# Row norms in a fused attention and MoE kernel: the power on GpSimd replaced by Newton steps on VectorE, in groups and taken ahead

## Chip, cores, metric

One core of one Trainium2 chip. The metric is the device time of one execution in microseconds (us).

## The reference

Cosine attention over 8 batches x 12 heads x 448 rows x 64, followed by a two-layer MoE with a quick GELU.

```python
q_n = q / (np.linalg.norm(q, axis=-1, keepdims=True) + 1e-06)
k_n = k / (np.linalg.norm(k, axis=-1, keepdims=True) + 1e-06)
scores = np.matmul(q_n, k_n.transpose(0, 1, 3, 2)) / tau
...                                   # softmax over the last axis, times v
h = x @ w_in                          # x: 3584 x 768, w_in: 768 x 2048
g = h * (1.0 / (1.0 + np.exp(-1.702 * h)))
out = g @ w_out                       # w_out: 2048 x 768
```

## The kernel before

The kernel works on 48 pairs of heads, six pairs a batch. A pair takes two "steps". TensorE gets, in each step, scores, a share of MoE matmuls of an earlier batch, attention times v, another share, transposes (in the second step of a pair), another share. An engine takes its instructions in order, so whatever is emitted ahead of an instruction on the same engine can hold it: in the profile before, VectorE waited 3.01 us for a power at 310 us and ran an eviction only behind it, at 313.72, though that eviction's matmuls had ended at 309.45. Names of tiles in the profiles: n are sums of squares, nrm, rs and (in the new kernel) y the norms and their reciprocals, qks the scaled q and k, vt the cast v; tps are transposes in PSUM and qkT their copy; sp are scores, expT their exponentials; avp is attention times v in PSUM and av its eviction, the copy out of PSUM; mm is the PSUM tile of the MoE matmuls, th and gT make the GELU. tps and avp share one PSUM buffer, so transposes can start only when the av before them has been evicted (28 waits of TensorE, 45.7 us, in the profile before). The norms:

```python
def norm(x):                                     # one pair
    nrm = p_n.tile([P, 2, 2, C], FP32, name="nrm")
    nc.gpsimd.tensor_tensor(out=nrm, in0=n2s.pop(x), in1=half_c[...], op=ALU.pow)
    nc.vector.tensor_scalar(out=nrm, in0=nrm, scalar1=1e-6, scalar2=None, op0=ALU.add)
    rss[x] = p_n.tile([P, 2, 2, C], FP32, name="rs")
    nc.vector.reciprocal(out=rss[x], in_=nrm)
# (cut: the sums of squares before it: Square on ScalarE, tensor_reduce on VectorE;
#  the scale behind it: q and k times rs, on GpSimd)
```

The softmax denominators take a way through DRAM. Three pairs together: `den_out` (rows of av to DRAM), `den_in` (back as a dense tile, dnm), `den_rcp` (reciprocal rcg on VectorE, out to DRAM as rcp, back broadcast over partitions as rcb), then `normalise` (xT = av times rcb, on VectorE). All these transfers, the loads of q, k and v, and the stores are issued from one queue, SP's. The weights are issued from GpSimd's queue.

```python
for x in range(NPAIR):
    at(2 * (x - 6), load_qk, x)
    ...
    at(2 * (x - 2), norm, x)
    at(2 * (x - 2) + 1, scale, x, 1)
    ...
    if x % HP == HP - 1:
        at(2 * (x + 1) + 1 + 2 * d + 2, queue_moe, x // HP)
for i in range(4):
    at(-1 + 2 * i, load_w_in, i)
    at(9 + 2 * i, load_w_out, i)
```

## Time and profile before

| | before |
|---|---|
| time, median | 625.45 us |
| VectorE waiting for the power on GpSimd | 141.6 us |
| head: until the first MoE matmuls run at full pace | 114.8 us |
| middle: until TensorE has finished seven batches of MoE | 463.9 us |
| tail: last batch | 49.2 us |

The profiled execution took 627.9 from first to last instruction, so the three stretches sum to 627.9. They are read from TensorE's timeline. A wait in the profile is put down to the engine and instruction whose end came last. Line numbers (L119) differ between the two kernels; the names of the tiles are the same.

### The profile page before, as it was taken

The numbers are of one execution on the slowest core, as the hardware profiler recorded it, in microseconds if no ns is written. First come the engines' busy times: TensorE is split into PE (matmuls) and PEld (weight loads), VectorE is DVE, ScalarE is ACT, GpSimd is POOL, SyncE is SP. The second block draws the span as 40 slices with busy tenths as digits, with TensorE's granted clock in tenths as the row PEclk, the third lists the DMA queues.
The fourth block names the chain that finished last, engine by engine and source line by source line (L and its number), as shares of the span: only waits on it lengthen the run. The fifth ranks groups of instructions, "written<-read, shape, count | busy, mean of one in ns | idle before, by whom it ended". The sixth has DMA issues, their size and how long they took to land.

```text
span 627.9 us, 7945 instructions
## 1 busy us (share of the span) xinstructions
PE 496.5 (79%) x2816; PEld 243.0 (39%) x2816; DVE 294.5 (47%) x593; ACT 310.3 (49%) x473; POOL 281.7 (45%) x254
## 2 busy tenths in 40 slices
PE   0575555779979896998679896989589896898897
PEld 0122122344534453444334453445234452344454
DVE  3333353574456634555456635554556535451420
ACT  3553534465546554674546553664456553551331
POOL 5867565454535463355544463355643553300000
PEclk9966757799979998999979997999989997899899
DMA  9885957031522243143412252143412320002002
GB/s 226 155 168 124 186 122 158 8 104 44 172 60 68 66 125 110 45 110 88 144 44 68 77 141 83 45 111 96 135 45 67 85 74 26 2 24 86 13 25 76
DMA packets 55431, 56.61 MB, mean 90 GB/s; under 512 B 8064, under 2 KB 51936, under 8 KB 55392
## 3 DMA queue, kind: packets, MB, share of 16 engines
q1 hardware_dynamic: 50144, 49.82, 28.4%
q0 software_dynamic: 5248, 6.29, 6.6%
q8 instruction: 22, 0.36, 0.2%
q14 instruction: 17, 0.14, 0.1%
HBM read 51.20 MB, written 11.18 MB: 99 GB/s over the span
## 4 chain that ended last, share of the span: by engine, by line
PE 47%; DVE 26%; POOL 19%; issue 4%; ACT 2%; DMA 1%; SPq 0%; DVEq 0%; POOLq 0%
POOL nrm L119 18%; PE mm L297 16%; PE mm L257 15%; DVE xT L242 8%; PE avp L192 6%; DVE av L200 6%; PE sp L170 6%; PE tps L153 4%; DVE n L113 4%; DVE gT L267 3%; ACT th L266 2%; DVE qkT L159 2%; DVE rs L129 2%; DVE nrm L125 1%; DMA rcb<-rcp 1%
## 5 line engine op out<-in xcount | busy, mean ns | idle before, releaser
L119 POOL TENSOR_TENSOR nrm<-n,half_c 112x16 f32<-112x16 f32 x48 | 139.2, 2899 | 226.9 <-DVE n L113 226.9
L257 PE MATMUL mm<-xT,w_in 128*128 128x448 f16 x768 | 180.3, 379 | 46.3 <-DVE xT L242 42.2
L182 ACT ACTIVATE expT<-sp 112x896 f16<-112x896 f32 x192 | 170.1, 913 | 92.6 <-PE sp L170 92.4
L297 PE MATMUL mm<-w_out,gT 128*128 128x384 f16 x896 | 160.9, 326 | 0.6 <-DVE gT L267 0.6
L266 ACT ACTIVATE th<-mm 128x448 f16<-128x448 f32 x128 | 69.5, 543 | 143.2 <-PE mm L257 142.3
L257 PEld LDWEIGHTS <-w_in 128*128 128x128 f16 x768 | 75.2, 103 | 92.7 <-issue 38.9
L267 DVE SCALAR_TENSOR_TENSOR gT<-th,mm 128x448 f16<-128x448 f16 x128 | 76.8, 612 | 71.5 <-ACT th L266 71.4
L297 PEld LDWEIGHTS <-gT 128*128 128x128 f16 x896 | 83.9, 98 | 66.5 <-issue 11.5
L192 PE MATMUL avp<-expT,vt 112*128 112x448 f16 x384 | 99.3, 385 | 0.0
L200 DVE TENSOR_SCALAR av<-avp 65x448 f16<-65x448 f32 x96 | 58.1, 605 | 63.5 <-PE avp L192 63.0
L170 PE MATMUL sp<-qkT 64*112 64x448 f16 x384 | 68.4, 437 | 23.3 <-DVE qkT L159 21.7
L153 PE MATMUL tps<-ident,qks 112*128 112x112 f16 x384 | 33.2, 242 | 56.8 <-DVE av L200 45.7
L125 DVE TENSOR_SCALAR nrm<-nrm 112x16 f32<-112x16 f32 x48 | 8.4, 175 | 141.6 <-POOL nrm L119 141.6
L153 PEld LDWEIGHTS <-qks 112*128 112x128 f16 x384 | 28.5, 113 | 110.8 <-issue 56.3
L135 POOL TENSOR_TENSOR qks<-k,rs 112x512 f16<-112x512 f32 x48 | 50.0, 1042 | 34.4 <-DVE rs L129 27.2
L113 DVE TENSOR_REDUCE n<-sq 112x8 f32<-112x512 f32 x96 | 64.2, 670 | 2.6 <-ACT sq L108 2.0
L305 ACT ACTIVATE ost<-mm 128x384 f32<-128x384 f32 x56 | 27.4, 490 | 71.3 <-PE mm L297 71.1
L242 DVE TENSOR_TENSOR xT<-av,rcb 64x448 f16<-64x448 f16 x96 | 57.1, 594 | 7.1 <-DMA rcb<-rcp 5.9
L192 PEld LDWEIGHTS <-vt 112*128 112x128 f16 x384 | 37.2, 103 | 47.1 <-issue 21.2
L135 POOL TENSOR_TENSOR qks<-q,rs 112x512 f16<-112x512 f32 x48 | 51.9, 1081 | 0.0
L170 PEld LDWEIGHTS <-qkT 64*112 64x112 f16 x384 | 20.0, 143 | 63.1 <-DVE qkT L159 31.5
L159 DVE COPY qkT<-tps 128x896 f16<-128x896 f16 x48 | 29.8, 620 | 17.8 <-PE tps L153 16.8
(19 smaller groups left out, 126.0 us busy)
## 6 DMA issues: line engine op xcount, KB each, us to landing
q<-in_q_dram SPq DMA_DIRECT2D x48, 224.0 KB
k<-in_k_dram SPq DMA_DIRECT2D x48, 224.0 KB
v<-in_v_dram SPq DMA_DIRECT2D x48, 224.0 KB
rcb<-rcp SPq DMA_DIRECT2D x32, 168.0 KB
w_in<-in_moe_w_in_dram POOLq DMA_DIRECT2D x4, 768.0 KB, 8.6
w_out<-in_moe_w_out_dram POOLq DMA_DIRECT2D x4, 768.0 KB, 7.6
out_dram<-ost SPq DMA_DIRECT2D x7, 336.0 KB
out_dram<-ost SPq DMA_DIRECT2D x8, 288.0 KB
```

What stands on the lines that cost most here:

```text
L113: nc.vector.tensor_reduce(out=n2s[x][:, ti], in_=sqs.pop((x, ti)), axis=AX.X, op=ALU.add)
L119: nc.gpsimd.tensor_tensor(out=nrm, in0=n2s.pop(x), in1=half_c[:P, :, None, None].to_broadcast((P, 2, 2, C)), op=ALU.pow,)
L135: nc.gpsimd.tensor_tensor(out=qkss[x][:, ti].rearrange("p c j d -> p j c d"), in0=src, in1=rss[x][:, ti, :, :, None].to_broadcast((P, 2, C ...
L153: nc.tensor.transpose(out=tps[:, ti, c * P : (c + 1) * P], in_=qks[:, ti, c].rearrange("p j d -> p (j d)"), identity=ident[:P, :P],)
L170: nc.tensor.matmul(out=sp[:, j, :S], lhsT=qkT[64 * j : 64 * (j + 1), 1, c * P : (c + 1) * P], rhs=qkT[64 * j : 64 * (j + 1), 0, :], start= ...
L182: nc.scalar.activation(out=e, in_=sps.pop((x, c))[:, :, :S], func=AF.Exp, scale=inv_tau, **kw)
L192: nc.tensor.matmul(out=ps, lhsT=vts[x % 4][:, c, j], rhs=exps[x, c][:, j], start=(c == 0), stop=(c == C - 1),)
L200: nc.vector.tensor_scalar(out=avs[x][:n, j], in0=ps[:n], scalar1=AV_SCALE, scalar2=None, op0=ALU.mult)
L242: nc.vector.tensor_tensor(out=xT[r], in0=av[r, j], in1=rcbs[x // GRP][r, x % GRP], op=ALU.mult)
L257: nc.tensor.matmul(out=ps[:, :S], lhsT=w_in_sb[:, kk, 128 * m : 128 * (m + 1)], rhs=xTs[b, kk], start=(kk == 0), stop=(kk == KT1 - 1),)
L267: nc.vector.scalar_tensor_tensor(out=gT[:, m], in0=th, scalar=1.0, in1=ps[:, :S], op0=ALU.add, op1=ALU.mult,)
L297: nc.tensor.matmul(out=ps[:, :NW], lhsT=gT[:, kk, 128 * t : 128 * (t + 1)], rhs=w_out_sb[:, kk, cols], start=(kk == 0), stop=(kk == KT2 - 1),)
```

## The change

Intent: take the power off GpSimd, so that VectorE need not wait; do the norms of three pairs in one block, several pairs ahead of use; spread MoE matmuls over the remaining steps.

```diff
-    def norm(x):
-        nc.gpsimd.tensor_tensor(out=nrm, in0=n2s.pop(x), in1=half_c[...], op=ALU.pow)
-        nc.vector.tensor_scalar(out=nrm, in0=nrm, scalar1=1e-6, ..., op0=ALU.add)
-        nc.vector.reciprocal(out=rss[x], in_=nrm)
+    def norm(grp):                                  # 1, 2 or 3 pairs
+        a = n2s.pop(grp).rearrange("p g a b c -> p (g a b c)")
+        nc.vector.tensor_scalar(out=y.bitcast(I32), in0=a.bitcast(I32),
+            scalar1=-0.5, scalar2=RS_MAGIC, op0=ALU.mult, op1=ALU.add)
+        for ca, cb in ((-RS_A, RS_B), (-0.5, 1.5)):
+            nc.vector.scalar_tensor_tensor(out=t, in0=y, scalar=ca, in1=y, ...)
+            nc.vector.tensor_tensor(out=t, in0=t, in1=a, op=ALU.mult)
+            nc.vector.scalar_tensor_tensor(out=y, in0=t, scalar=cb, in1=y, ...)
+        nc.vector.tensor_scalar(out=t, in0=y, scalar1=1e-6, scalar2=1.0, ...)
+        nc.vector.reciprocal(out=t, in_=t)
+        nc.vector.tensor_tensor(out=y, in0=y, in1=t, op=ALU.mult)
 (cut)
-        at(2 * (x - 6), load_qk, x)
-            at(2 * (x - 3) + ti, square, x, ti)
-        at(2 * (x - 2), norm, x)
+        s = sq_step.get(x, 2 * (x - 6))            # squares three pairs earlier
+        if x >= HP:
+            at(s - 5, load_qk, x)
+        if x == group_of[x][-1]:
+            at(s + (1 if x < HP else 2), norm, group_of[x])
 (cut)
-        at(-1 + 2 * i, load_w_in, i)
-        at(9 + 2 * i, load_w_out, i)
+        at(3 + 2 * i, load_w_in, i)
+        at(11 + 2 * i, load_w_out, i)
 (cut: the first six pairs' loads before the loop, one scale moved to VectorE)
-        jobs = later.pop(s, [])
+        jobs = sorted(later.pop(s, []), key=...)   # squares, reduces, norms first
+        step_ns = max(todo / max(2 * NPAIR + 4 - s, 1), 0)     # was 3150
```

The first of the ten operations reads the bits of the fp32 sum as an integer and makes a first guess of one over the square root; two rounds of three operations (Newton steps) refine it; the last three bring in the 1e-6.

More of the change, by code (lines that the diff above doesn't have):

```diff
@@ L10 @@
 FP16 = mybir.dt.float16
+I32 = mybir.dt.int32
 AF = mybir.ActivationFunctionType
@@ L16 @@
 MM2_NS = 163
-STEP_NS = 3150
+RS_MAGIC = float(0x5F1FFFF9)
+RS_A, RS_B = 0.703952253, 0.703952253 * 2.38924456
 AV_SCALE = 2.0**-11
@@ L74 @@
     ctx.enter_context(tc.manual_schedule())
-    half_c = const.tile([128, 2], FP32)
-    nc.vector.memset(half_c, 0.5)
     ident = const.tile([128, 128], FP16)
@@ L110, in reduce, with scale @@
     def reduce(x, ti):
-        if ti == 0:
-            n2s[x] = p_n.tile([P, 2, 2, C], FP32, name="n2")
+        grp = group_of[x]
+        if grp not in n2s:
+            n2s[grp] = p_n.tile([P, len(grp), 2, 2, C], FP32, name=f"n2_{len(grp)}")
         nc.vector.tensor_reduce(
-            out=n2s[x][:, ti], in_=sqs.pop((x, ti)), axis=AX.X, op=ALU.add
-        )
-    def norm(x):
-        nrm = p_n.tile([P, 2, 2, C], FP32, name="nrm")
-        nc.gpsimd.tensor_tensor(
-            out=nrm,
-            in0=n2s.pop(x),
-            in1=half_c[:P, :, None, None].to_broadcast((P, 2, 2, C)),
-            op=ALU.pow,
-        )
+            out=n2s[grp][:, x - grp[0], ti],
+            in_=sqs.pop((x, ti)),
+            axis=AX.X,
+            op=ALU.add,
+        )
+    def norm(grp):
+        n = len(grp)
+        a = n2s.pop(grp).rearrange("p g a b c -> p (g a b c)")
+        y = p_n.tile([P, 16 * n], FP32, name=f"y_{n}")
+        t = p_n.tile([P, 16 * n], FP32, name=f"t_{n}")
+        nc.vector.tensor_scalar(
+            out=y.bitcast(I32),
+            in0=a.bitcast(I32),
+            scalar1=-0.5,
+            scalar2=RS_MAGIC,
+            op0=ALU.mult,
+            op1=ALU.add,
+        )
+        for ca, cb in ((-RS_A, RS_B), (-0.5, 1.5)):
+            nc.vector.scalar_tensor_tensor(
+                out=t, in0=y, scalar=ca, in1=y, op0=ALU.mult, op1=ALU.mult
+            )
+            nc.vector.tensor_tensor(out=t, in0=t, in1=a, op=ALU.mult)
+            nc.vector.scalar_tensor_tensor(
+                out=y, in0=t, scalar=cb, in1=y, op0=ALU.add, op1=ALU.mult
+            )
         nc.vector.tensor_scalar(
-            out=nrm, in0=nrm, scalar1=1e-6, scalar2=None, op0=ALU.add
+            out=t, in0=y, scalar1=1e-6, scalar2=1.0, op0=ALU.mult, op1=ALU.add
         )
-        rss[x] = p_n.tile([P, 2, 2, C], FP32, name="rs")
-        nc.vector.reciprocal(out=rss[x], in_=nrm)
-    def scale(x, ti):
+        nc.vector.reciprocal(out=t, in_=t)
+        nc.vector.tensor_tensor(out=y, in0=y, in1=t, op=ALU.mult)
+        yv = y.rearrange("p (g a b c) -> p g a b c", g=n, a=2, b=2)
+        for x in grp:
+            rss[x] = yv[:, x - grp[0]]
+    def scale(x, ti, eng=None):
         if x not in qkss:
@@ L134, in scale @@
         src = (q32, k32)[ti].pop(x)
-        nc.gpsimd.tensor_tensor(
+        (eng or nc.gpsimd).tensor_tensor(
             out=qkss[x][:, ti].rearrange("p c j d -> p j c d"),
@@ L314 @@
     streams = []
+    todo = (B - 1) * (KT1 * KT2 * MM1_NS + 7 * KT2 * MM2_NS)
     def fill(ns):
+        nonlocal todo
         while ns > 0 and streams:
             try:
-                ns -= next(streams[0])
+                n = next(streams[0])
+                ns -= n
+                todo -= n
             except StopIteration:
@@ L345, in at @@
         later.setdefault(s, []).append((f, a))
+    sq_step = {0: -4, 1: -3, 2: -2, 3: 0, 4: 2, 5: 3, 6: 5, 7: 6, 8: 7, 9: 9, 10: 10, 11: 11}
+    groups = [(0,), (1, 2), (3, 4), (5,)]
+    groups += [tuple(range(g, g + GRP)) for g in range(HP, NPAIR, GRP)]
+    group_of = {x: g for g in groups for x in g}
     for x in range(NPAIR):
-        at(2 * (x - 6), load_qk, x)
-        at(2 * (x - 5), load_v, x)
-        for ti in range(2):
-            at(2 * (x - 3) + ti, square, x, ti)
-            at(2 * (x - 3) + ti + 1, reduce, x, ti)
-        at(2 * (x - 2), norm, x)
+        s = sq_step.get(x, 2 * (x - 6))
+        if x >= HP:
+            at(s - 5, load_qk, x)
+            at(2 * (x - 4), load_v, x)
+        for ti in (1, 0):
+            late = 0 if x < HP or ti == 1 else 1
+            at(s + late, square, x, ti)
+            at(s + late + (1 if x > 0 else 0), reduce, x, ti)
+        if x == group_of[x][-1]:
+            at(s + (1 if x < HP else 2), norm, group_of[x])
         at(2 * (x - 2) + 1, scale, x, 1)
-        at(2 * (x - 2) + 1, scale, x, 0)
+        at(2 * (x - 2) + 1, scale, x, 0, *([nc.vector] if x == 0 else []))
         at(2 * (x - 2) + 1, cast_v, x)
@@ L368 @@
     for i in range(4):
-        at(-1 + 2 * i, load_w_in, i)
-        at(9 + 2 * i, load_w_out, i)
+        at(3 + 2 * i, load_w_in, i)
+        at(11 + 2 * i, load_w_out, i)
+    for x in range(HP + 2):
+        if x < HP:
+            load_qk(x)
+        if x >= 2:
+            load_v(x - 2)
     make_identity(nc, ident)
@@ L380 @@
         x, half = s // 2, s % 2
-        jobs = later.pop(s, [])
+        jobs = sorted(
+            later.pop(s, []), key=lambda j: {square: 0, reduce: 1, norm: 2}.get(j[0], 3)
+        )
+        step_ns = max(todo / max(2 * NPAIR + 4 - s, 1), 0)
         if 0 <= x < NPAIR:
@@ L384 @@
             exp(x, 2 * half)
-        fill(STEP_NS * 0.33)
+        fill(step_ns * 0.33)
         if 0 <= x < NPAIR:
@@ L391 @@
             f(*a)
-        fill(STEP_NS * 0.33)
+        fill(step_ns * 0.33)
         if half == 1 and 0 <= x + 1 < NPAIR:
@@ L396 @@
             f(*a)
-        fill(STEP_NS * 0.34)
+        fill(step_ns * 0.34)
     fill(1e9)
```

## The prediction

> **What bounds the kernel now.** I read the waits summed over the whole run first, because the change removes one wait.
>
> ```profile
> POOL nrm L119 <- DVE n L113: 226.9, 46, 9.5
> DVE nrm L125 <- POOL nrm L119: 141.6, 48, 5.1
> PE tps L153 <- DVE av L200: 45.7, 28, 4.5
> PE mm L257 <- DVE xT L242: 42.2, 10, 6.1
> ```
>
> The power on GpSimd waits 226.9 us for its sums of squares, so GpSimd is not full. It matters because VectorE waits for it: 48 waits, 141.6 us, about 2.95 us each, the length of one power. VectorE takes its instructions in order, so whatever stands behind that wait stands still too. The timeline near 310 us shows it:
>
> ```profile
> 310.41 2.90 POOL L119 TENSOR_TENSOR nrm<-n,half_c 112x16 f32<-112x16 f32 x1 [3.28 <-DVE n L113]
> ...
> 313.34 0.17 DVE L125 TENSOR_SCALAR nrm<-nrm 112x16 f32<-112x16 f32 x1 [3.01 <-POOL nrm L119]
> 313.55 0.25 DVE L129 RECIPROCAL rs<-nrm 112x16 f32<-112x16 f32 x1
> 313.72 0.56 DVE L200 TENSOR_SCALAR av<-avp 128x448 f16<-128x448 f32 x1
> ...
> 314.20 2.27 DVE L242 TENSOR_TENSOR xT<-av,rcb 64x448 f16<-64x448 f16 x2
> ...
> 316.53 0.53 PE L257 MATMUL mm<-xT,w_in 128*128 128x448 f16 x1 [6.13 <-DVE xT L242]
> ```
>
> A PSUM eviction (av) and two normalisations (xT), ready earlier, run only after the power, and TensorE loses 6.13 us. The chain of waits agrees: the power alone is 18.1% of it (114 us). Next, stretches of 20 us (columns: engine busy us, granted clock, DMA share, GB/s):
>
> ```profile
> 40.00:60.00 20.00, 11.45 (x54) 4.46 (x54) 7.66 (x18) 8.97 (x12) 12.92 (x12) 0.62 0.66 147
> 220.00:240.00 20.00, 20.00 (x134) 10.73 (x133) 7.82 (x18) 11.87 (x19) 10.53 (x10) 1.00 0.45 128
> 300.00:320.00 20.00, 11.79 (x69) 5.50 (x67) 10.42 (x21) 8.47 (x13) 11.55 (x10) 0.86 0.37 107
> 580.00:600.00 20.00, 17.00 (x80) 8.29 (x80) 9.81 (x19) 7.06 (x13) 0.00 (x0) 0.91 0.06 22
> ```
>
> These are three regimes. In the head (to the first MoE matmul at 115 us) there is attention alone: no engine is full, and a pair takes 9.5 us. In the middle, stretches of the second MoE matmul beside attention fill TensorE completely, while stretches around the start of the first MoE matmul do not. The tail is the last batch's MoE on TensorE.
>
> [...]the power takes 2,899 ns for 16 elements a partition, a tensor_scalar of the same shape 175 ns. [...]here tensor_scalar to reciprocal starts 0.21 us apart (313.34 to 313.55), so about full length each.[...]
>
> **The change, part by part.**
>
> *Removed.* 48 powers: 139.2 us of GpSimd (281.7 falls to some 141), and the 141.6 us of VectorE waits. The 96 small VectorE operations go too (8.4 + 12.1 = 20.5 us).
>
> *Added.* Ten small VectorE operations a group, 18 groups: 14 of three pairs, two of two, two of one. [...]The reciprocal measures 253 ns at 16 elements and 289 at 24 (fp16), so 4.5 ns an element, some 397 ns at 48 (estimate). [...]for one pair 9 x 0.175 + 0.253 = 1.83[...]. VectorE goes from 294.5 to 294.5 - 20.5 + 39 + 0.6 (one scale moved to it) = about 314 us. They wait only for VectorE itself, and from the seventh pair on lie three to four pairs ahead of their use, so nobody waits for their result[...].
>
> *Moved.* Squares and loads go earlier, the weights later. *The balanced MoE share does next to nothing*: the instruction order of TensorE shows the same 18 first or 21 second MoE matmuls a step (half a pair) in both kernels up to step 89. The loop runs on until its nanoseconds are used up, and 1,050 or 1,040 ns both mean six of 189 or seven of 163. Only from step 90 are there 19 instead of 18. I give it 0 to 1 us.
>
> **Head: 115 to about 80 us.** First scores come at 16.2 us now; loads and the two-pair group still stand ahead of the first qkT copy, so about 15. Then 9.5 pairs to the first MoE step. A pair needs of ScalarE 4 x 0.913 + 2 x 0.627 = 4.9 us; of VectorE 2 x 0.67 + 2 x 0.605 + 0.62 + 2 x 0.594 + 0.85 = 5.2 us; of TensorE at the low clock about 6.2 us (1.00 per four scores, 1.6 per four attends, 0.92 for transposes). So about 6.3 us instead of 9.5: 15 + 60 = 75. DMA is the check:
>
> ```profile
> q1 hardware_dynamic: 12788, 11.52, 36.4%
> q0 software_dynamic: 5248, 6.29, 34.5%
> ```
>
> That is the DMA view of the first 120 us: plain loads 0.364 x 120 / 11.52 = 3.8 us a MB, weights 41 us in all. By the first MoE step the new order wants q and k of 16 pairs and v of 12 (10.1 MB, 38 us) and has asked for all weights: 79 us. So DMA takes over as the limit of the head at nearly the same place. I take 80, a gain of 35.
>
> **Middle: 464 to about 410 us** (115.0 to 578.7, where TensorE runs out of the seventh batch). Floor of TensorE from full stretches: four scores 0.52, four attends 0.76, eight transposes 0.39 in two steps, MoE matmuls 0.190 and 0.164 us. A batch of 12 steps: 12 x 1.28 + 6 x 0.39 = 17.7, plus 96 x 0.190 + 112 x 0.164 = 36.6: 54.3 us against 70 now (the xT groups before the first MoE matmul repeat at 244.8, 314.3, 385.0, 454.4). Seven batches of MoE and 79 steps of attention: 256 + 116 = 372. Now 92 us are lost beyond that. I keep 38: per batch 2.5 us for the first MoE matmul waiting on the last xT (in the same step, behind a reduce), 1.5 for a norm block that falls into it, 0.8 of clock; and 4 us for the steps with no or hardly any MoE (51, 52, 75, 76), whose order is unchanged. A step of the first MoE matmul needs 6 x 3 x 0.19 + 1.47 = 4.9 us of TensorE and about 4.5 of VectorE (three gT of 0.61, a reduce, an eviction, half a copy, one xT[...]), so VectorE has little slack there. That is why I keep as much.
>
> **Tail: 49 us, unchanged**: five of waiting on the last denominators' way through DRAM, 44 of MoE.
>
> Sum 80 + 410 + 49 = 539 on the profiled run; the timed runs lie 2 us under the profile's span. **Prediction 537 us**, 14% under 625.45.
>
> **Rivals.** *(1) VectorE becomes the bound.* For: 4.5 of 4.9 us a step in the first MoE phase, and the blocks come in bursts. Against: it is 47% busy over all and idles in the second phase (7.82 of 20). If it ruled those phases, losses would be nearer 65 us: about 565. *(2) The head is held by transfers*: weights now sit in 14 steps that run faster; 0.82 to 1.00 DMA share in 20 to 100 us says it can happen. If plain loads starve behind weights, the head is 90 to 95: about 550. *(3) The power was only one of parallel waits*, so evictions and normalisations still keep TensorE waiting, and the low clock stays in the head: 9.5 falls only to 7.5 us a pair, middle losses 60: about 575. *(4) All goes well*: losses of 15 to 20 us, head 72: about 510. Full stretches such as 220 to 240 speak for it.
>
> **Range and chances.** Head 72 to 92, middle 390 to 435, tail 47 to 53; not all at the same end: 512 to 566 holds 8 in 10. To miss 2% (613) would need nearly all of the gain to turn into a new wait, so faster 0.97, same 0.02, slower 0.01.
>
> **What would show it.** GpSimd busy near 141 us and no long wait of VectorE on it;[...] VectorE busy near 314. First MoE matmul at 75 to 90 us, with DMA share near full before it. A batch taking 58 to 61 us instead of 70. TensorE's granted clock above 0.93 in the middle. The remaining waits of TensorE on xT at 2 to 3 us instead of 6. I am wrong if the head stays above 95 us, if the batch period stays above 64 us, or if VectorE waits on DMA or ScalarE take the place of the power.

What the prediction said of the hardware without a trace of this case behind it is cut out of it, and the cuts are marked. Terms of its sums are gone with it, namely the durations of VectorE's operations over two and three pairs. The ten operations came to 39 us over the whole run, the 39 in 294.5 - 20.5 + 39 + 0.6, and the about 4.5 us of VectorE a step holds a share of them. The changed kernel measured 41 us in all, 2.28 us for the ten operations of a block of three pairs, and 208 ns for one of its two-input operations.

## The result

560.18 us median (559.58 to 561.48, 4 runs) against 625.53 us (4 runs) beside it. The ratio is 0.8956, 95% interval 0.8927 to 0.8985. A ratio is the mean time of one kernel's fast runs over that of the other's of the same rounds, so it is not quite the ratio of the medians.

| | before | forecast | after |
|---|---|---|---|
| head, us | 114.8 | 80 | 106.3 |
| middle, us | 463.9 | 410 | 400.3 |
| tail, us | 49.2 | 49 | 51.2 |
| GpSimd busy, us | 281.7 | 141 | 140.7 |
| VectorE busy, us | 294.5 | 314 | 303.2 |

The waits summed over the run, kernel after (us in total, times, longest us):

```profile
POOL qks L156 <- DVE y L147: 170.8, 18, 13.8
POOL vt L167 <- PE avp L213: 124.7, 47, 4.4
DVE av L221 <- PE avp L213: 111.5, 51, 4.0
...
PE mm L278 <- DVE xT L263: 18.6, 14, 4.7
...
DVE xT L263 <- DMA rcb<-rcp: 13.1, 4, 5.5
```

VectorE's 141.6 us of waiting for GpSimd are gone. GpSimd now waits for VectorE (170.8 us) and TensorE (124.7), and runs ahead all the same: TensorE waited for its scales once, 10.1 us before the first transposes. The matmul's wait on xT fell from 42.2 us to 18.6. One line is small in the sum and large in one place: xT waits for the transfer rcb, 13.1 us in four waits against 5.9 in two before; 7.5 of them now lie in the head. Three stretches of 20 us (busy us of TensorE's matmuls, its weight loads, VectorE, ScalarE and GpSimd; granted clock, DMA share, GB/s) show where:

```profile
40.00:60.00 20.00, 13.98 (x62) 4.76 (x61) 10.82 (x25) 14.10 (x21) 6.22 (x8) 0.74 0.83 172
60.00:80.00 20.00, 5.87 (x32) 2.63 (x31) 9.92 (x25) 6.19 (x10) 5.16 (x9) 0.66 1.04 215
...
220.00:240.00 20.00, 17.98 (x109) 8.62 (x109) 14.29 (x33) 13.23 (x22) 5.12 (x7) 1.00 0.23 69
```

In the middle, from 120 to 500 us, TensorE is now busy 95% of the time (82 to 100% in stretches of 20 us), at the full clock in all but one of them (0.91). The stretch from 60 to 80 us has TensorE busy for only 5.87 us, with the DMA engines full (share 1.04). The timeline there, kernel after:

```profile
60.69 0.81 POOL L363 DMA_DIRECT2D w_out<-in_moe_w_out_dram  x1
...
65.35 1.35 SPq L250 DMA_DIRECT2D rcb<-rcp  x2
...
66.01 0.81 POOL L363 DMA_DIRECT2D w_out<-in_moe_w_out_dram  x1
...
71.85 0.38 DVE L263 TENSOR_TENSOR xT<-av,rcb 64x448 f16<-64x448 f16 x1 [5.53 <-DMA rcb<-rcp]
...
75.43 0.62 DVE L221 TENSOR_SCALAR av<-avp 128x448 f16<-128x448 f32 x1
...
76.10 0.90 PE L174 MATMUL tps<-ident,qks 112*128 112x112 f16 x8 [9.26 <-DVE av L221]
...
79.78 1.61 DVE L263 TENSOR_TENSOR xT<-av,rcb 64x448 f16<-64x448 f16 x2
81.42 0.62 DVE L180 COPY qkT<-tps 128x896 f16<-128x896 f16 x1
82.10 0.99 PE L191 MATMUL sp<-qkT 64*112 64x448 f16 x4 [5.09 <-DVE qkT L180]
```

Two quarters of w_out are asked for around the moment that the first rcb is. The delay had begun a transfer earlier: SP's queue stood 6.7 us for rcp before it could ask for rcb. VectorE stands for rcb (5.53 and 1.97 us), the eviction av stands behind xT, and TensorE loses 9.26 us. It loses 5.09 more before the scores, because two reduces, a norm block (77.28 to 79.86) and two more xT stand ahead of the qkT copy. Scores of successive pairs begin at 14.5, 19.3, 29.2, 39.1, 46.0, 55.0, 62.4, 82.1, 89.2 and 94.7 us. So periods without a disturbance are about 7.1 us (6.9, 7.4, 7.1). Those with a block of norms ahead of the qkT copy or of an eviction are 10.0, 9.9 and 9.1. The one with the stall, which has a norm block too, is 19.7. The first (4.8) and the last (5.5) are shorter.

### The profile page after: what moved, and what is told of

It reads as the page before. It is cut to its first block, busy times and chain, and to the rows that moved or that the text cites. A ratio compares the mean times of both kernels' runs of the same rounds, so it can differ in the third digit from the quotient of the medians.

```text
span 557.8 us, 7958 instructions
## 1 busy us (share of the span) xinstructions
PE 474.8 (85%) x2816; PEld 236.2 (42%) x2816; DVE 303.2 (54%) x677; ACT 310.5 (56%) x473; POOL 140.7 (25%) x205
## 4 chain that ended last, share of the span: by engine, by line
PE 65%; DVE 18%; DMA 10%; issue 2%; ACT 2%; SPq 2%; DVEq 0%; ACTq 0%
PE mm L318 23%; PE mm L278 21%; PE avp L213 12%; PE sp L191 8%; DVE xT L263 4%; DVE av L221 3%; DVE n L114 3%; DMA rcp<-rcg 3%; DMA rcb<-rcp 3%; DVE qkT L180 2%; DMA v<-in_v_dram 2%; DVE gT L288 2%; PE tps L174 2%; ACT th L287 2%; DMA q<-in_q_dram 1%
## 5 line engine op out<-in xcount | busy, mean ns | idle before, releaser
L278 PE MATMUL mm<-xT,w_in 128*128 128x448 f16 x768 | 170.2, 362 | 18.6 <-DVE xT L263 18.6
L278 PEld LDWEIGHTS <-w_in 128*128 128x128 f16 x768 | 72.4, 99 | 86.8 <-issue 29.5
L156 POOL TENSOR_TENSOR qks<-k,y 112x512 f16<-112x512 f32 x48 | 50.5, 1053 | 188.4 <-DVE y L147 170.8
L191 PE MATMUL sp<-qkT 64*112 64x448 f16 x384 | 64.2, 411 | 28.6 <-DVE qkT L180 25.5
L167 POOL CAST vt<-v 112x256 f16<-112x256 f32 x96 | 37.2, 401 | 130.8 <-PE avp L213 124.7
L174 PE MATMUL tps<-ident,qks 112*128 112x112 f16 x384 | 28.9, 223 | 31.1 <-DVE av L221 21.1
L156 POOL TENSOR_TENSOR qks<-q,y 112x512 f16<-112x512 f32 x47 | 49.2, 1048 | 0.0
L174 PEld LDWEIGHTS <-qks 112*128 112x128 f16 x384 | 25.3, 103 | 54.0 <-issue 39.3
L263 DVE TENSOR_TENSOR xT<-av,rcb 64x448 f16<-64x448 f16 x96 | 39.3, 409 | 14.7 <-DMA rcb<-rcp 13.1
L108 ACT ACTIVATE sq<-k 112x512 f32<-112x512 f32 x48 | 30.3, 632 | 6.7 <-DMA k<-in_k_dram 5.2
## 6 DMA issues: line engine op xcount, KB each, us to landing
w_out<-in_moe_w_out_dram POOLq DMA_DIRECT2D x4, 768.0 KB, 10.1
```

Source lines behind the costliest of these rows:

```text
L156: (eng or nc.gpsimd).tensor_tensor(out=qkss[x][:, ti].rearrange("p c j d -> p j c d"), in0=src, in1=rss[x][:, ti, :, :, None].to_broadcast ...
L174: nc.tensor.transpose(out=tps[:, ti, c * P : (c + 1) * P], in_=qks[:, ti, c].rearrange("p j d -> p (j d)"), identity=ident[:P, :P],)
L191: nc.tensor.matmul(out=sp[:, j, :S], lhsT=qkT[64 * j : 64 * (j + 1), 1, c * P : (c + 1) * P], rhs=qkT[64 * j : 64 * (j + 1), 0, :], start= ...
L263: nc.vector.tensor_tensor(out=xT[r], in0=av[r, j], in1=rcbs[x // GRP][r, x % GRP], op=ALU.mult)
L278: nc.tensor.matmul(out=ps[:, :S], lhsT=w_in_sb[:, kk, 128 * m : 128 * (m + 1)], rhs=xTs[b, kk], start=(kk == 0), stop=(kk == KT1 - 1),)
```

## The experiments

Two theories of the head stood at first. T: transfers, the weights above all, are in the way of rcb. V: the order on VectorE holds it, with norm blocks in a phase in which TensorE has no MoE matmuls to fill with. A second question was what the middle owes to which part of the change. "Head" and "middle" are as in the table, from each run's profile.

| run | time, us | ratio to before | head, us | middle, us |
|---|---|---|---|---|
| changed kernel | 560.2 | 0.896 | 106.3 | 400.3 |
| e1 weights by memset (wrong result) | 558.5 | 0.893 | 105.1 | 400.4 |
| e2 weights as before | 560.6 | 0.896 | 108.2 | 400.3 |
| e3 first normalise late | 557.4 | 0.892 | 111.1 | 399.5 |
| e4 Newton in place | 579.2 | 0.926 | 96.3 | 431.9 |
| e5 quarter of the weights (wrong result) | 555.1 | 0.888 | 101.6 | 399.8 |
| e6 reduces behind the copy | 561.3 | 0.898 | 108.8 | 399.3 |
| e7 norms pair by pair, ahead | 588.6 | 0.941 | 112.4 | 424.4 |
| e8 power ahead | 639.1 | 1.021 | 127.8 | 454.4 |
| e9 fixed share | 561.0 | 0.897 | 108.3 | 400.5 |
| e10 power ahead, 10 input buffers | 556.5 | 0.890 | 108.0 | 395.9 |
| e11 head rearranged | 553.9 | 0.886 | 101.4 | 400.5 |
| e12 the same as e11, 10 input buffers | did not build | | | |
| e12b the same as e11, 9 input buffers | 554.8 | 0.887 | 101.9 | 400.5 |

The profiled run of e3 took 562.9 us, over 5 us more than the median, so its head is not typical.

### e1, e5: weights without transfers

```diff
 e1:
-        nc.gpsimd.dma_start(out=w_in_sb[:, :, n], in_=moe_w_in...)
+        nc.gpsimd.memset(w_in_sb[:, :, n], 0.03)          # w_out likewise
 e5:
-    w_in_sb = wpool.tile([128, KT1, DFF], FP16, name="w_in")
+    w_in_sb = wpool.tile([128, KT1, 512], FP16, name="w_in")
-                    lhsT=w_in_sb[:, kk, 128 * m : 128 * (m + 1)],
+                    lhsT=w_in_sb[:, kk, 128 * (m % 4) : 128 * (m % 4 + 1)],
                                        # w_out likewise; one load of each, not four
```

> The changed kernel with both weights filled by GpSimd memsets instead of transfers (wrong result on purpose; the memsets cost GpSimd some 2 to 3 us each, eight of them). Theory T, transfers: 41 us of weight transfers crowd the head, the first rcb lands late and VectorE stands for it in order (9.3 us of TensorE idle at 66 to 76 us). Then the first MoE matmuls reach full pace at 85 us or earlier instead of 106, and the whole takes about 540 us. Theory V, VectorE's order: reduces and norm blocks stand ahead of evictions and qkT copies in a phase where TensorE has no filler, whatever the DMA does. Then full pace comes at 100 us or later and the whole takes 554 or more.

> The changed kernel with a quarter of each weight loaded and used four times over (wrong result on purpose; no engine gets extra work, unlike the memsets of e1, which kept GpSimd busy and once held a small VectorE operation for 5.8 us). Theory T: weight transfers hold the head through the late rcb (pair period 19.7 us instead of 7.1 around 62 to 82 us). Then full pace of the first MoE matmul comes at 95 us or before instead of 106, and the whole takes 546 to 550 us. Theory V: VectorE's order holds it anyway. Then 103 us or later, 557 or more.

e1 hardly moved (558.5 us), but it was not clean. Its timeline, VectorE and GpSimd alone:

```profile
31.88 2.66 POOL L357 MEMSET w_in<- 128x3072 f16 x1
...
34.05 5.81 DVE L127 TENSOR_SCALAR y<-n 112x16 int32<-112x16 int32 x1
...
34.50 1.05 POOL L156 TENSOR_TENSOR qks<-k,y 112x512 f16<-112x512 f32 x1
35.50 1.05 POOL L156 TENSOR_TENSOR qks<-q,y 112x512 f16<-112x512 f32 x1
...
36.48 0.75 POOL L167 CAST vt<-v 112x256 f16<-112x256 f32 x2
...
37.16 2.66 POOL L357 MEMSET w_in<- 128x3072 f16 x1
```

An operation that took 0.17 us with GpSimd idle (at 6.24 us in the changed kernel) took 5.81 us. A memset (2.66 us) was running when it began; then GpSimd went through two scales, two casts and a memset without a gap. The operation ended (39.86) when the last memset did (39.82). The memsets kept GpSimd busy and so made a cost of their own. By what means GpSimd held the operation was not shown.

e5 gives no engine extra work. It came to 555.1 us, head 101.6. So three quarters of the weights' transfers cost the head about 5 us, and V's 557 and T's 550 are both missed: T is right in kind and small in size. Its timeline shows the rest of the stall:

```profile
67.54 0.38 DVE L263 TENSOR_TENSOR xT<-av,rcb 64x448 f16<-64x448 f16 x1 [0.31 <-DMA rcb<-rcp]
68.30 1.19 DVE L263 TENSOR_TENSOR xT<-av,rcb 64x448 f16<-64x448 f16 x3 [0.37 <-DMA rcb<-rcp]
69.51 0.62 DVE L221 TENSOR_SCALAR av<-avp 128x448 f16<-128x448 f32 x1
...
70.19 0.55 PE L174 MATMUL tps<-ident,qks 112*128 112x112 f16 x8 [2.35 <-DVE av L221]
...
75.35 1.00 PE L191 MATMUL sp<-qkT 64*112 64x448 f16 x4 [4.61 <-DVE qkT L180]
```

VectorE waits 0.7 us for rcb here, and the pair (62.8 to 75.35 us) still takes 12.6 us instead of 7.1. So of the stall's 19.7 us about 7 are the late transfers, and 5.5 are VectorE's own order: six xT and a norm block ahead of an eviction and a copy.

### e2, e3, e11: when weights and the first normalisation come

```diff
 e2:
-        at(3 + 2 * i, load_w_in, i)
-        at(11 + 2 * i, load_w_out, i)
+        at(-1 + 2 * i, load_w_in, i)
+        at(9 + 2 * i, load_w_out, i)
 e3 (p_av from 6 to 10 buffers):
-                at(s + 2 * d + 1 + i // 2, normalise, x - GRP + 1 + i)
+                at(s + 2 * d + 1 + i // 2 + (5 if x < GRP else 0), normalise, ...)
 e11 = e3 and:
+        at(-1 + 2 * i, load_w_in, i)
+        at((6, 7, 20, 22)[i], load_w_out, i)
```

> The changed kernel with the weights asked for at the steps of the kernel before (w_in from step -1, w_out from step 9), so 4 and 2 steps earlier. Theory T with room: DMA stood idle from 27 to 33 us, earlier weights use that, fewer of them stand in front of the first rcb: 546 to 556 us. Theory V, or T with DMA full anyway: within 3 us of 560. Worse than 560 if early weights delay q and k.

> The changed kernel with the normalisation of the first three pairs five steps later (nobody needs them before the first MoE matmul) and 10 buffers of av so that they can wait. Theory T as an in-order wait: the 5.5 + 2.0 us of VectorE waiting on rcb at 66 to 74 us, with the 9.3 us gap of TensorE, leave: 549 to 554 us. If the transfers limit the head by their sheer volume, the time comes back as waits of ScalarE on q and k or GpSimd on v: 558 or more.

> The changed kernel with weights kept away from the first denominators (w_in from step -1 as before, two quarters of w_out at steps 6 and 7, the other two at 20 and 22), and the first normalisation late, with 10 buffers of av. If late rcb and dnm transfers behind weights, and VectorE's wait for them in order, are what the head lost against the forecast of 80 us: the stall of 12.6 us and most of the 5 us of the run with quarter weights leave, full pace of the first MoE matmul at 90 to 94 us, 544 to 549 us. If the head's serial order and norm blocks limit it: 553 or more.

Earlier weights alone do nothing (560.6 us, as V, or T with DMA full, expected): the pair with the stall still takes 20.6 us, since quarters of w_out still lie around the first rcb. The late normalisation alone brings 557.4 us with a wide interval (0.887 to 0.898), short of the 549 to 554 expected. Its profile shows that pair at 10.1 us, but the next group's denominators then came late:

```profile
87.94 0.30 DVE L245 RECIPROCAL rcg<-dnm 112x24 f16<-112x24 f16 x1 [7.04 <-DMA dnm<-den]
```

VectorE stood 7.04 us for dnm instead. The wait had found another transfer of the same chain. Both edits together, with the weights kept clear of the denominators, take the stall away: the pair periods from 58 us on are 7.0, 9.3 (with a norm block), 6.9 and 6.9 us. The time is 553.9 us, and the head 101.4. That is the lowest median of all runs, with a correct result. It is above the 544 to 549 expected for late transfers, and fits the 553 or more expected for serial order and norm blocks. Of the 10.4 us that this pair gained, 2.8 came back in the pair that now starts at 46.3 us, where VectorE waits 2.04 us for the first dnm, and 1.5 each in the last pair and between it and full pace. What is left in the head is for the most part not this stall.

### e6: norm blocks behind the copy

```diff
-        for f, a in jobs[: len(jobs) // 2]:
+        cut = len(jobs) // 2 if s >= 19 else 0
+        for f, a in jobs[:cut]:
```

> The changed kernel with all side jobs of steps before 19 (reduces, norm blocks, scales) behind the transposes and the qkT copy instead of half of them ahead. Theory V: pair periods of 9.9, 9.9 and 9.1 us around the norm blocks of the head fall towards the 7.1 us of pairs without one, together 7 to 9 us: 551 to 554 us. Theory T: the stall on rcb takes the gain back: 558 or more.

561.3 us, no gain. The first scores came 2.9 us earlier (11.6), but a later norm block met GpSimd's scales and weight issues and took from 30.3 to 35.7 us instead of about 2; three of the operations in it took 0.91 to 1.07 us beside GpSimd, where 0.17 was usual. One period grew to 13 us, and the stall on rcb stayed (19.2 us). So the run does not tell what the norm blocks cost in a clean head. That stays open.

### e4, e7: Newton without the rest, and without the grouping

e4 is the kernel before with the ten VectorE operations in place of the power, pair by pair; e7 is the changed kernel with single pairs from the seventh on:

```diff
 e7:
-    groups += [tuple(range(g, g + GRP)) for g in range(HP, NPAIR, GRP)]
+    groups += [(g,) for g in range(HP, NPAIR)]
```

> The kernel before with the power replaced by the exponent guess and two Newton steps on VectorE, pair by pair and in the old place; loads, squares, weights and MoE share stay as before. If the wait for the power was the cost and taking the norms ahead in threes adds little: 570 us or less, with VectorE busy about 294 - 20 + 88 - some 18 of faster xT = 344 us. If taking ahead and grouping carry half of the gain: 590 or more.

> The changed kernel with the norms from the seventh pair on taken pair by pair, still ahead: 42 blocks of 1.83 us instead of 14 of 2.3, so VectorE gets 45 us more. If VectorE has slack in the middle and being ahead is what counts: 563 us or less. If VectorE is close to the bound beside the first MoE matmul: 567 to 577, that is 1 to 2.5 us a batch, and grouping is what counts.

e4: 579.2 us, between the two expectations. Its middle is 431.9 us; the Newton steps in the old place already bring 32 of the middle's 64 us, and the head falls to 96.3, lower than in the changed kernel. VectorE was busy for 363.7 us, not the 344 expected, because xT stayed at 0.587 us. The head: nine pair periods take 72.2 us there against 80.2 in the changed kernel, and VectorE does not wait for rcb, although all weights are loaded and more had been moved by 66 us (13.7 MB against 11.4). So the weights alone do not make the stall. The loads of q, k and v, the squares and the norm blocks differ as well, and no run separates them, nor does one join this head to the grouped norms of the middle. e7: 588.6 us, worse than expected, middle 424.4. VectorE has some 48 us more work than in the changed kernel (351.4 against 303.2), and the middle is 24 us longer. So VectorE is close enough to being the limit that half of its extra work shows, and the grouping is worth those 24 us. Between e4 and e7 (ahead or in place, both single pairs) the middle differs by only 7.5 us.

### e8, e10: the power again, but ahead

Groups of three on GpSimd, with VectorE's two operations taken two steps later from the tenth pair on:

```diff
+        nc.gpsimd.tensor_tensor(out=t, in0=a, in1=half_c[...], op=ALU.pow)   # norm
+        ...                                                    # norm_b, two steps on
+        nc.vector.tensor_scalar(out=t, in0=t, scalar1=1e-6, ..., op0=ALU.add)
+        nc.vector.reciprocal(out=y, in_=t)
 e10 = e8 and:
-    p_in = pool("p_in", 6)
+    p_in = pool("p_in", 10)
```

> The changed kernel with the power on GpSimd again, for the groups of three, and the two VectorE operations behind it taken two steps later (from the tenth pair on), so that VectorE need not stand for it. If the wait in VectorE's order was the whole cost of the power: within 12 us of the changed kernel, 560 to 572. If the power as such costs, by holding scales on GpSimd (some 8.5 us for 48 elements) or VectorE's two-input operations (xT at 0.59 us instead of 0.41): 580 or more.

> The run with the power ahead (e8, 639 us) with 10 instead of 6 input buffers. There the load queue waited 210 us for GpSimd, whose scales stood behind 8 us powers, and so the denominators' transfers behind it came late and VectorE waited 77 us on them. Theory B, the wait moved into the load queue: with free buffers the queue no longer waits, and the time falls to 565 to 580 us. Theory P, the power itself: still 610 or more.

e8: 639.1 us, 1.6 to 2.5% slower than the kernel before, and far above the 560 to 572 expected if VectorE's wait was the whole cost of the power. VectorE no longer waits for the power for long. It waits for a transfer, and the load queue waits for GpSimd. From the waits of e8, first VectorE's, then the load queue's own:

```profile
DVE rcg L239 <- DMA dnm<-den: 77.0, 13, 14.1
```

```profile
SPq L95 <- POOL vt L161: 209.8, 17, 19.3
```

A power over 48 elements takes 8.0 us. The scales stand behind it on GpSimd, the input buffers come free late, the load that wants one blocks the SP queue, and the denominators' transfers stand behind that load. e10 tests this by adding buffers alone. The time fell by 83 us to 556.5, below the 565 to 580 expected. In the load queue's waits of e10, that of L95 on GpSimd is gone, and VectorE's on dnm fell from 77.0 us to one wait:

```profile
DVE rcg L239 <- DMA dnm<-den: 3.5, 1, 3.5
```

The chain is shown. The run also shows more: with the wait removed at both ends (but for 26.5 us of VectorE on the power, in five waits at the head's first groups), the power on GpSimd is as fast as the Newton steps. Its row in e10, by form:

```profile
L129 POOL TENSOR_TENSOR t<-n,half_c 112x48 f32<-112x48 f32 x14 | 112.1, 8010 | 171.6 <-DVE n L116 171.6
```

112.1 us of powers over three pairs are there, and the middle is 395.9 us.

### e12b: the control for the buffers

> The rearranged head (e11, 553.9 us, Newton steps on VectorE) with 9 instead of 6 input buffers (10 do not fit beside the 10 av buffers); nothing else differs. A control for the run with the power ahead and 10 input buffers (556.5 us). If buffers help only where GpSimd is slow to free them, this is within 2 us of 554 (the load queue waits for GpSimd only some 9 us in all in the changed kernel), and the power ahead is then as fast as the Newton steps. If the buffers alone speed up the Newton version as well: 550 or less, and the comparison of the two was unfair by that much.

```diff
 e12b = e11 and:
-    p_in = pool("p_in", 6)
+    p_in = pool("p_in", 9)
```

e12, with 10 input buffers beside e11's 10 av buffers, did not build: the on-chip memory was too small (the last pool wanted 9 kB a partition, 5.47 were left). e12b has 9: 554.8 us against 553.9, within the 2 us expected. More input buffers do nothing for the Newton version, so e10 against the changed kernel (0.890 against 0.896) is a fair comparison. The difference seems real, though small: e9 below, the changed kernel but for the MoE share, ran in the same rounds as e10 and took 559.4 to 561.9 us, e10 555.9 to 558.3. What makes it was not tested.

### e9: the fixed share

```diff
-        step_ns = max(todo / max(2 * NPAIR + 4 - s, 1), 0)
+        step_ns = 3150
```

> The changed kernel with the fixed MoE share of 3,150 ns a step in place of the balanced one. TensorE's instruction order is the same up to step 89, so within 2 us of the changed kernel's 560. If the balancing carries anything: 565 or more.

561.0 us, as expected: the balancing carries nothing.

## Why the prediction was right, and where it missed

The total lay inside the range, and the mechanism of the middle was right. Part of the first is luck: the head missed by 26 us, beyond its own range of 72 to 92 and beyond the text's sign of being wrong (a head above 95), while the middle came out 10 us better than forecast.

- **The bound before.** Right. VectorE's in-order wait for the power was the cost, not GpSimd's work. e10 shows it from the other side: the power may stay where nobody ready stands behind it (112.1 us of powers over three pairs, VectorE's wait for them down from 141.6 to 26.5 us, 556.5 us in all).
- **Durations.** Right. The three-pair block's two-input operations took 208 ns, the first and the eighth, with one input, 184 and 188, and its reciprocal 453 ns (397 forecast: the slope came from an fp16 reciprocal, 4.5 ns an element, where fp32 has 6.3). All norm operations come to some 41 us (39 forecast), and GpSimd to 140.7 us (141).
- **VectorE at 314 us.** It was 303.2. The miss is the normalisation xT, taken over unchanged at 0.594 us; it fell to 0.409, or 17.8 us in all, of which others took some back. A slow instance before (2.27 us for two at 314 us) stood beside GpSimd's scales. It is not the power that slows xT: it takes 0.587 us in e4, without a power, and 0.386 in e8, with it.
- **Middle, 410 us.** 400.3: a batch takes 60.0 us (a block of first MoE matmuls recurs two batches on, at 223.8 and 343.8), inside 58 to 61. TensorE's waits on xT come to 8.0 us in all from 130 to 480 us, 1.7 at the longest; the forecast kept 2.5 a batch for them. The granted clock is 1.00 in nearly all of it, against 0.93 and more.
- **"They wait only for VectorE itself ... nobody waits for their result".** True of TensorE and VectorE in the middle; GpSimd's scales waited for the norms (117.3 us from 130 to 480 us), ahead of need. Grouping proved to be worth 24 us (e7), more than the text made of it.
- **"The balanced MoE share does next to nothing".** Right (e9).
- **Tail, 49 us.** 51.2.
- **From profile to timed run.** "2 us under the profile's span" was misread: the profiled execution before took 629.85 us, 2 us above its span, as did the one after (559.58 and 557.8). This is 4 of the 23 us between 537 and 560.
- **Head, 80 us: wrong by 26.** Four terms of that sum were mis-sized. First, "about 6.3 us instead of 9.5" a pair: undisturbed pairs took 7.1, because TensorE, in order and without filler, stands open for the eviction ahead of the transposes (0.7 us) and for the qkT copy behind them (0.7 to 1.2); over nine pairs 7 us. Second, the norm blocks, of which the text said that nobody waits for their result: in the head they stood in the series of eviction, transposes, copy and scores, and three pairs were 2.0 to 2.9 us longer, 7.6 us. Third, "DMA takes over as the limit of the head at nearly the same place": the volume did not set the time, a place did. One pair took 12.6 us more than an undisturbed one, about 7 of it for late transfers and 5.5 for six xT and a norm block in VectorE's order (e5). Fourth, the last scores to full pace took 11.6 us instead of half a period of 3.2, 8.4 us more, with VectorE doing a norm block and the xT in a row; the kernel before already needed 12.8 there. Two pairs were 3.9 us faster than 7.1, the allowance for DMA was 5, and the start 0.5 better: 7 + 7.6 + 12.6 + 8.4 - 3.9 - 5 - 0.5 = 26. The experiments settle the stall's part (e5, e11: 5 to 6 us off the total; in e11 the rest came back elsewhere). That the blocks and the serial order make up the remainder is read from the timeline; e6 failed to show it.
- **The rivals.** Rival 2, the head held by transfers at 90 to 95 us and about 550 us in all, came closest in kind, but its mechanism was starved plain loads, and the run shows the small denominators' transfers late instead. (The text took its DMA share from 20 to 100 us as 0.82 to 1.00; its view had 0.66 to 1.00.) Rival 3's head, 7.5 us a pair, was near the 7.1 of undisturbed pairs; its middle was not. Rival 1 was half true: VectorE is near being the limit in the middle (e7), but not at it in the changed kernel.

## What to carry to other kernels

Before replacing a slow operation, ask who stands in order behind its wait; moving the wait to where nobody ready stands behind it was worth as much here as a faster operation (e10, 556.5 us, against 560.2), and moving it carelessly let it return in a queue far away (e8: 209.8 us in loads, then 77.0 on transfers of denominators). Count what a queue's first blocked entry holds up, and give it buffers before giving up an engine (e8 to e10: 639.1 to 556.5 us). A phase without filler work must be summed as a series of dependent pieces, and not as the busiest engine's load (here 7.1 us a pair against 6.3).

## What the runs measured of single operations

- GpSimd's power: 2,924 ns for 16 elements a partition, 5,416 for 32 and 8,005 for 48 (e8), about 160 ns an element.
- VectorE's fp32 reciprocal: 252 ns at 16 elements, 354 at 32, 453 at 48 (changed kernel), so 6.3 ns an element. Its two-input fp32 operations: 174 ns at 16, 191 at 32, 208 at 48 (the same), so about 1.1 ns an element.
- A small VectorE operation beside a busy GpSimd: in e1 one was recorded for 5.81 us, across five GpSimd instructions that began after it, where 0.17 us was usual.
- The power on GpSimd against the Newton steps on VectorE: with an 8.0 us power in place of a VectorE block of some 2.3 us, the run was as fast (e10, 556.5 us against 560.2).
